# First block of a fused linear-attention and two-MLP kernel: weight decoding by steps, state update and split behind it, unit 4 begun in front of the block

## The chip, the cores and the metric

The kernel runs on one core of one Trainium2 chip. The metric is the device time of one execution in microseconds (us). Three runs of the kernel before took 947.99, 950.5 and 950.2 us, a median of 950.2 us.

## The reference

A recurrent linear attention is followed by two MLPs, in fp32:

```
state = 0                                    # [4 batches, 8 heads, 48, 48]
for t in range(768):
    y[t]  = r[t] @ (state + (u * k[t]) x v[t])
    state = w[t] * state + k[t] x v[t]       # w in 0.8 .. 0.95
x = y as [3072 tokens, 384]
h = x @ w_in;   x = elu(h) @ w_out           # 384 -> 2048 -> 384
h = x @ w_in2;  out = silu(h) @ w_out2       # 384 -> 2048 -> 384
```

## The kernel before

**Attention.** The 3072 tokens are cut into 24 units of 128 tokens (6 chunks of time by 4 batches). For each unit, VectorE (DVE) makes running products of w with two scans (`scan`, L160, and `scan_back`, L170), the product r*k (`products`, L222), and scaled copies of r and k (`q`, L237, and `kt`, L244). ScalarE (ACT) writes a check sum of the decays (`far`, L178), a copy of the whole decay (`whole_decay`, L183) and the diagonal of the attention matrix (`diag`, eight activations, L201, from the sums that `summed` takes on TensorE, L229). TensorE (PE) then makes the scores (`scores`, L287, two banks of PSUM), a transposed k (`ktok`, L253, copied out by ACT in `ktok_copy`, L259), the contribution of the old state (`past`, L342), the outer product for the new state (`outer`, L316) and the part within the unit (`within`, L361). DVE masks the scores (`masked`, L304). `update` brings the state forward (DVE L326 and L328, then ACT L330), and `split` writes the unit's output as two rounded parts xh (ACT L373) and xl (DVE L374).

**MLPs.** Weights and activations are held as a rounded part and a remainder, so each product is three matmuls. The first MLP runs in six blocks of four units (512 tokens); a block has 16 slots, one for each slice of 128 hidden channels. A slot f (function `slot`) issues nine matmuls into a bank `ph` (`hidden`, L443), the split of the slot before (gh on ACT L465, gl on DVE L466), the exponential and a ReLU on ACT (L450, L452), one half of a tick, g = max(...) on DVE (L459), the nine output matmuls of slot f-2 (`flush_out`, L474), and the other half of the tick. The banks `ph` are two, so the hidden matmuls of slot f+2 wait for g of slot f.

**Weights.** They come in as 64-bit floats and are decoded by hand in four steps for each slice: `w_load` (two DMAs of 384 KB into one of three staging buffers), `w_scale` (two activations, L405 and L407), `w_join` (two DVE operations, L414 and L416) and `w_split` (wh on ACT L428, wl on DVE L429). The first MLP's 16 slices are decoded during the first block: `w_tick` does a join and a scale in the first half of a slot, a split and a load in the second.

**Order.** All engines work through queues that the program writes by hand (`manual_schedule`). `dense_units` does units 0 to 3 with nothing beside them; while it runs, slices 0 to 2 are decoded. It ends with eight transposes that only keep PE busy (`keep_clock`, L617). The first block then runs, and its slots carry units 4 to 7, each as six steps (`round_ticks`: t0 to t5) spread over the half slots. Unit 4 is in `ALONE`: its preparation stands in `prep_rest`, in the first two half slots. In t5 of a unit stand past, outer, within, the next unit's ktok, then update, split and ktok_copy. The three remaining banks of PSUM go around between these: the scores of unit n+1 are written to the banks that the state update and the ktok_copy of unit n read.

Of the kernel before, what the change touches and what calls it, by code (L numbers as in the profile page):

```python
# [34 lines left out]
def kernel(  # L35
# [116 lines left out]
    def prep_steps(n):  # L152
# [61 lines left out]
        def products():  # L214
            if n >= SUMMED:
                return
            if n < BLOCKS[0]:
                rk = g_p.tile([RB, NP, L], F32, tag="gh", name="rk")
            else:
                rk = st["af"][0:RB, 0:NP * L].rearrange("p (j t) -> p j t", j=NP)  # L220
            st["rk"] = rk
            nc.vector.tensor_tensor(out=rk, in0=st["c"][:, 0], in1=st["c"][:, 1], op=ALU.mult)  # L222
# [165 lines left out]
    wh, wl = {}, {}  # L388
    halves, loaded, scaled, whole = [], [], [], []

# [28 lines left out]

    def w_split():  # L420
        if whole:
# [5 lines left out]
            h, l = (x.rearrange("p o c -> p (o c)") for x in (h, l))  # L427
            nc.scalar.activation(out=h, in_=t, func=ACTF.Copy)  # L428
            nc.vector.tensor_tensor(out=l, in0=t, in1=h.bitcast(F32), op=ALU.subtract)  # L429

# [105 lines left out]
    def round_parts(n, free=None):  # L536
# [11 lines left out]
        return pe, do  # L548

    def round_ticks(n):  # L550
        pe, do = round_parts(n)
# [35 lines left out]
        def t5():  # L587

            pe["past"]()
            pe["outer"]()  # L590
            pe["within"]()
            do("ktok")
            pe["update"]()
            pe["split"]()
            do("ktok_copy")
            load_unit(n + 2, "v")

        return [t0, t1, t2, t3, t4, t5]

    def dense_units():  # L600

# [4 lines left out]
                 for pool, tag, k in ((ps_o, "o", 3), (ps_h, "h", 2)) for _ in range(k)]  # L606
        sums_p = banks[2]

        def begin(n):
# [9 lines left out]
        for n in range(-1, count):  # L619
# [5 lines left out]
            if more:  # L625
# [6 lines left out]
                p["whole_decay"]()  # L632
                p["far"]()
                p["q"]()
                p["kt"]()
# [5 lines left out]
            if more:  # L641
                begin(n + 1)
                w_join()
            if n >= 0:
                pe[n]["masked"](0)
                pe[n]["masked"](1)
# [6 lines left out]
            if more:  # L653
                w_split()
                w_load()
# [7 lines left out]
            if n == KRAT:  # L663
                nc.sync.dma_start(u_sb, u.rearrange("h d -> (h d)").unsqueeze(0).to_broadcast([128, H * D]))
        keep_clock(8)
        pe[count - 1]["split"]()
        w_join()
        w_split()
        w_load()
        w_scale()  # L670
        pe[count - 1]["update"]()

    def prep_rest(at, n, p):

        if at == 1:
            p["bonus"]()
# [46 lines left out]
    def w_tick(part):  # L723

        if part == 0:
            w_join()
            w_scale()
        else:
            w_split()
            w_load()  # L730

    with tc.manual_schedule():
# [10 lines left out]
        setup()  # L743
        nc.scalar.activation(out=upper, in_=above_sb, func=ACTF.Copy)
        dense_units()

# [11 lines left out]
        for j, units in enumerate(BLOCKS):  # L758
            nt, final = units * L, j == len(BLOCKS) - 1
            ticks = [] if final else list(range(FIRST[j + 1], FIRST[j + 2]))  # L760
            todo, count, at = [], 6 * len(ticks), 0
            alone = prep_steps(ticks[0]) if ticks and ticks[0] in ALONE else None

            def tick(part):
# [5 lines left out]
                wait, end = DELAY if alone else 0, END if j == 0 else 2 * NF - 2  # L770
                while done < count and done * (end - wait) < (at - wait) * count:
                    if not todo:
                        todo.extend(round_ticks(ticks.pop(0)))
                    todo.pop(0)()
                    done += 1
                if j == 0 or final and f % 4 != 3:
                    w_tick(part)

            for f in range(NF):
# [112 lines left out]
    def all_weights(m):  # L892
        stage_open(2)
        w_start(m)
        for _ in range(NF):
            w_scale()
            w_join()
            w_split()
            w_load()
# [92 lines left out]
```

## Time and profile before

| what | value |
|---|---|
| runs of the kernel | 947.99, 950.5, 950.2 us; median 950.2 us |
| the profiled execution | 947.38 us, of which the span of the trace is 945.6 us |
| mean granted clock of PE | 0.981 |
| busy share of the span | PE 97%, DVE 52%, ACT 53%, POOL 14% |
| chain that ended last | PE 89%, DVE 6%, DMA 2%, ACT 2% |

Times within the trace count from the span's start. The dense units fill about the first 42.5 us, and the first block follows. In a timeline row the two leading numbers are start and duration; what stands in brackets is the idle time of the engine before it and what ended it. An operation's successor on the same engine can start a little before the operation's recorded end.

### The profile page before, as it was taken

The page shows a single profiled execution, that of the slowest core. Times are in us where ns is not written, and L with a number is a line of the kernel's source. Part 1 is how long each engine was busy: PE and PEld are TensorE (multiplying, and loading weights), DVE is VectorE, ACT ScalarE, POOL GpSimd, SP SyncE. Part 2 cuts the span into 40 slices and gives each one's busy share as a digit, 9 for nine tenths or more (in the row PEclk, how much of TensorE's full clock was granted, in tenths as well). Part 3 has the DMA queues.
Part 4 walks back from the last instruction along what each step waited for, and adds up shares of the span by engine and source line. Part 5 has one row for each costly group of instructions (what it writes and reads, how often), then busy time and mean ns, then how long its engine had stood idle before and what let it go on. Part 6 is the DMA issues. An engine that isn't in the chain of part 4 may idle for free.

```text
span 945.6 us, 15205 instructions
## 1 busy us (share of the span) xinstructions
PE 918.1 (97%) x6158; PEld 790.8 (84%) x6158; DVE 489.4 (52%) x726; ACT 502.4 (53%) x901; POOL 133.9 (14%) x101
## 2 busy tenths in 40 slices
PE   7779899999999999999999999999999999999996
PEld 7667688888888888888888899999999999999996
DVE  7798877776666776666378762212212212222211
ACT  6788866665655655555488963323323333333332
POOL 0000012443453334453000000000000000000000
PEclk8799999999999999999999999999999999999998
DMA  8644414222322221220245330100200200200001
GB/s 252 184 153 161 163 48 124 69 67 57 110 67 73 91 66 57 78 68 1 101 141 193 136 99 1 67 0 1 68 1 1 68 1 1 67 1 1 34 1 37
DMA packets 32222, 68.69 MB, mean 73 GB/s; under 512 B 3600, under 2 KB 13968, under 8 KB 32144
## 3 DMA queue, kind: packets, MB, share of 16 engines
q1 hardware_dynamic: 32144, 67.64, 22.5%
q8 instruction: 50, 0.82, 0.4%
q14 instruction: 28, 0.23, 0.1%
HBM read 58.19 MB, written 9.44 MB: 72 GB/s over the span
## 4 chain that ended last, share of the span: by engine, by line
PE 89%; DVE 6%; DMA 2%; ACT 2%; issue 1%; SPq 0%; DVEq 0%; ACTq 0%
PE ph L443 40%; PE po L482 21%; PE po L474 19%; PE sc L295 2%; PE y L361 2%; PE y L342 1%; DVE wst L414 1%; PE ktp L253 1%; DVE wl L429 1%; DVE wst L416 1%; DMA in_v<-in_v_tok_dram 1%; DVE am L304 1%; DVE gl L466 1%; PE upd L316 1%; DMA above_sb<-in_above_dram 1%
## 5 line engine op out<-in xcount | busy, mean ns | idle before, releaser
L466 DVE TENSOR_TENSOR gl<-g,gh 128x512 fp32r<-128x512 f32 x192 | 144.8, 754 | 313.5 <-ACT gh L465 313.3
L443 PE MATMUL ph<-xh,wh 128*128 128x512 f32 x576 | 227.6, 395 | 2.1 <-DVE g L459 2.1
L443 PE MATMUL ph<-xh,wl 128*128 128x512 f32 x576 | 227.4, 395 | 0.0
L443 PE MATMUL ph<-xl,wh 128*128 128x512 f32 x576 | 227.2, 394 | 0.0
L465 ACT ACTIVATE gh<-g 128x512 fp32r<-128x512 f32 x192 | 120.8, 629 | 153.7 <-PE po L482 109.7
L454 ACT ACTIVATE g<-ph 128x512 f32<-128x512 f32 x96 | 57.4, 598 | 137.8 <-PE ph L443 137.1
L482 PE MATMUL po<-wh,gl 128*128 128x384 f32 x384 | 129.5, 337 | 0.0
L482 PE MATMUL po<-wh,gh 128*128 128x384 f32 x384 | 129.3, 337 | 0.0
L482 PE MATMUL po<-wl,gh 128*128 128x384 f32 x384 | 128.9, 336 | 0.0
L443 PEld LDWEIGHTS ph<-xh,wl 128*128 128x128 f32 x576 | 108.7, 189 | 23.5
L443 PEld LDWEIGHTS ph<-xh,wh 128*128 128x128 f32 x576 | 109.1, 189 | 22.4 <-DVE g L459 2.5
L443 PEld LDWEIGHTS ph<-xl,wh 128*128 128x128 f32 x576 | 108.8, 189 | 19.5
L474 PE MATMUL po<-gh,wh 128*128 128x512 f32 x288 | 114.7, 398 | 0.0
L474 PE MATMUL po<-gl,wh 128*128 128x512 f32 x288 | 113.0, 392 | 0.0
L474 PE MATMUL po<-gh,wl 128*128 128x512 f32 x288 | 112.7, 391 | 0.0
L450 ACT ACTIVATE g<-ph 128x512 f32<-128x512 f32 x96 | 56.5, 589 | 52.2 <-PE ph L443 52.1
L459 DVE SCALAR_TENSOR_TENSOR g<-g,ph 128x512 f32<-128x512 f32 x96 | 65.4, 681 | 27.7 <-ACT g L452 27.1
L482 PEld LDWEIGHTS po<-wh,gh 128*128 128x128 f32 x384 | 72.2, 188 | 4.3 <-ACT x2s L493 0.2
L482 PEld LDWEIGHTS po<-wl,gh 128*128 128x128 f32 x384 | 72.1, 188 | 4.1
L482 PEld LDWEIGHTS po<-wh,gl 128*128 128x128 f32 x384 | 72.0, 188 | 0.0
L233 POOL TENSOR_TENSOR ql<-tq,qh 64x512 fp32r<-64x512 f32 (+1 forms) x30 | 42.7, 1423 | 167.1 <-ACT qh L232 166.0
L474 PEld LDWEIGHTS po<-gh,wh 128*128 128x128 f32 x288 | 54.5, 189 | 11.8 <-issue 0.8
(92 smaller groups left out, 1078.6 us busy)
## 6 DMA issues: line engine op xcount, KB each, us to landing
wst<-in_moe_w_in_dram SPq DMA_DIRECT2D x32, 384.0 KB, 3.2
wst<-in_moe_w_out_dram SPq DMA_DIRECT2D x32, 384.0 KB, 4.0
in_c<-in_rk_ch_dram SPq DMA_DIRECT2D x24, 448.0 KB, 3.8
in_w<-in_w_ch_dram SPq DMA_DIRECT2D x24, 226.2 KB, 2.7
in_v<-in_v_tok_dram SPq DMA_DIRECT2D x24, 224.0 KB, 3.1
x_d<-x2s SPq DMA_DIRECT2D x18, 256.0 KB, 2.4
xl<-x_d SPq DMA_DIRECT2D x6, 768.0 KB, 5.3
out_dram<-os SPq DMA_DIRECT2D x24, 192.0 KB, 2.0
```

Of the source, the lines that this page charges most:

```text
L233: nc.gpsimd.tensor_tensor(out=lo, in0=x, in1=hi.bitcast(F32), op=ALU.subtract)
L253: nc.tensor.transpose(p[:, j, :], st["kd"][:, j, :], ident[0:RB, 0:RB])
L295: nc.tensor.matmul(p[:, jj].rearrange("p e t -> p (e t)"), a[:, j, :], b[:, j].rearrange("p e t -> p (e t)"), start=i == 0, stop=i == len( ...
L361: nc.tensor.matmul(y[32 * base:32 * base + 32, blk // 4, :], vf[:, c:c + 32], st["a"][:, h // 2, h % 2, :], start=not ch and step == 0, st ...
L443: nc.tensor.matmul(ph, lhs, xt[rhs][:, kt, 0:nt], start=n == 0, stop=n == 3 * KT - 1)
L450: nc.scalar.activation(out=g, in_=ph, func=ACTF.Exp)
L454: nc.scalar.activation(out=g, in_=ph, func=ACTF.Silu)
L459: nc.vector.scalar_tensor_tensor(out=g, in0=g, scalar=-1.0, in1=ph, op0=ALU.mult, op1=ALU.max)
L465: nc.scalar.activation(out=gh, in_=g, func=ACTF.Copy)
L466: nc.vector.tensor_tensor(out=gl, in0=g, in1=gh.bitcast(F32), op=ALU.subtract)
L474: nc.tensor.matmul(po[ot][:, 0:nt], lhs, rhs, start=f == 0 and i == 0, stop=f == NF - 1 and i == 2)
L482: nc.tensor.matmul(po[t][:, 0:DM], lhs[:, sl], rhs["o", f], start=f == 0 and i == 0, stop=f == NF - 1 and i == 2)
```

## The change

1. **Weights.** `w_split` is cut into `w_high` (wh on ACT) and `w_low` (wl on DVE). In the first half of slot f, `w_tick` now does wh of slice f+2, the join of slice f+3, wl of slice f+2 and a load; in the second half it scales slice f+4. The slice that was split at the end of `dense_units` (slice 2) is split in slot 0; the load that followed it goes there too.
2. **Update and split.** The end of t5 (update, split, ktok_copy and a load of v) becomes a step t6 that is put off to the end of the same half slot, behind `w_tick`.
3. **Unit 4.** Its products, scan and sums stand in `dense_units` in front of the masking of unit 3, its scan_back and whole_decay behind `keep_clock`. Of its preparation only q, kt, far and diag stay in the first two half slots.
4. **Mask.** The copy that turns the loaded mask into `upper` on ACT moves from before the dense units to behind the `far` of unit 0.

```diff
-            if n < BLOCKS[0]:
+            if n <= BLOCKS[0]:
                 rk = g_p.tile([RB, NP, L], F32, tag="gh", name="rk")
...
-    def w_split():
+    def w_high():
...
             nc.scalar.activation(out=h, in_=t, func=ACTF.Copy)
+            rounded_w.append((t, h, l))
+
+    def w_low():
+        if rounded_w:
+            t, h, l = rounded_w.pop(0)
             nc.vector.tensor_tensor(out=l, in0=t, in1=h.bitcast(F32), op=ALU.subtract)
...
+    behind = []
+
+    def follow():
+        while behind:
+            behind.pop(0)()
...
             do("ktok")
+            behind.append(t6)
+
+        def t6():
             pe["update"]()
             pe["split"]()
             do("ktok_copy")
...
+                if n == -1:
+                    mask()
                 p["q"]()
...
+            if n == count - 1:
+                after["bonus"]()
+                after["products"]()
+                after["scan"]()
+                after["summed"](sums_p[:, count * H:(count + 1) * H])
             if n >= 0:
                 pe[n]["masked"](0)
...
         keep_clock(8)
+        after["scan_back"]()
+        after["whole_decay"]()
         pe[count - 1]["split"]()
         w_join()
-        w_split()
-        w_load()
         w_scale()
         pe[count - 1]["update"]()
...
+        if n == BLOCKS[0]:
+            if at == 1:
+                p["q"]()
+                p["kt"]()
+                load_unit(n + 2, "wc")
+                p["far"]()
+                p["diag"](0)
+            elif at == 2:
+                p["diag"](1)
...
         if part == 0:
+            w_high()
             w_join()
+            w_low()
+            w_load()
+        else:
             w_scale()
-        else:
-            w_split()
-            w_load()
...
                 while done < count and done * (end - wait) < (at - wait) * count:
+                    follow()
...
                 if j == 0 or final and f % 4 != 3:
                     w_tick(part)
+                follow()
```

DVE at the end of the dense units and in slot 0 (slice 2 is `wst_220`, slice 3 `wst_297`; unit 4's scans write `both_100`, its q and kt are `tq` and `tk`). Before, from wl of slice 2 to q of unit 4:

```order
L429 TENSOR_TENSOR wl2_0_575<-wst_220,wh2_0_574 128x768
L328 TENSOR_TENSOR packed3_108<-upd_522,whole_432 112x192
L222 TENSOR_TENSOR am_599<-in_c_338 112x512
L159 MEMSET seed_99 112x4
L160 SCALAR_TENSOR_TENSOR both_100<-in_w_336,seed_99 112x516
L166 TENSOR_SCALAR seed_99<-both_100 112x4
L168 RECIPROCAL seed_99<-seed_99 112x4
L170 SCALAR_TENSOR_TENSOR both_100<-in_w_336,seed_99 112x515
L414 SCALAR_TENSOR_TENSOR wst_297<-wst_297 128x768
L416 SCALAR_TENSOR_TENSOR wst_297<-wst_297 128x768
L459 SCALAR_TENSOR_TENSOR g_596<-g_596,ph_586 128x512
L237 TENSOR_TENSOR tq_620<-in_c_338,both_100 112x512
```

In the changed kernel, the same stretch:

```order
L328 TENSOR_TENSOR packed3_108<-upd_522,whole_432 112x192
L237 TENSOR_TENSOR tq_606<-in_c_338,both_100 112x512
L244 TENSOR_TENSOR tk_608<-in_c_338,both_100 112x512
L414 SCALAR_TENSOR_TENSOR wst_297<-wst_297 128x768
L416 SCALAR_TENSOR_TENSOR wst_297<-wst_297 128x768
L434 TENSOR_TENSOR wl2_0_622<-wst_220,wh2_0_621 128x768
L464 SCALAR_TENSOR_TENSOR g_603<-g_603,ph_593 128x512
L471 TENSOR_TENSOR gl_648<-g_603,gh_647 128x512
```

The product and both scans of unit 4 have left the stretch, and wl of slice 2 stands between the join of slice 3 and g of slot 0.

ACT in slot 0 of the changed kernel (the first row is the end of unit 3's state update, the next two the exponential and ReLU of slot 0; `am_539` is unit 4's diagonal and, in the fourth row, the scrap output of its check sum):

```order
L330 ACTIVATE state3_104<-packed3_108 48x4x48 x2
L455 ACTIVATE g_603<-ph_593 128x512
L457 ACTIVATE g_603<-g_603 128x512
L178 ACTIVATE am_539,sums_98<-both_100 112x1031
L198 ACTIVATE dg_615<-early_160 128x8
L201 ACTIVATE am_539<-ident_94,dg_615 128x128 x4
L428 ACTIVATE wh2_0_621<-wst_220 128x768
L201 ACTIVATE am_539<-ident_94,dg_615 128x128 x4
L405 ACTIVATE wst_399<-wst_399 128x768
L407 ACTIVATE wst_399<-wst_399 128x768
L470 ACTIVATE gh_647<-g_603 128x512
```

Before, wh of slice 2 stood in front of that state update; now five operations of slot 0 and unit 4 stand between.

DVE in slot 10, where t5 of unit 6 falls in the first half (`packed2_107` is its state, `xl` its split). Before:

```order
L466 TENSOR_TENSOR gl_1254<-g_1214,gh_1253 128x512
L326 TENSOR_TENSOR packed2_107<-upd_1273,packed2_107 112x192
L328 TENSOR_TENSOR packed2_107<-packed2_107,whole_915 112x192
L374 TENSOR_TENSOR xl_662<-y_1260,xh_661 128x3x128
L414 SCALAR_TENSOR_TENSOR wst_1084<-wst_1084 128x768
L416 SCALAR_TENSOR_TENSOR wst_1084<-wst_1084 128x768
```

In the changed kernel:

```order
L471 TENSOR_TENSOR gl_1250<-g_1207,gh_1249 128x512
L414 SCALAR_TENSOR_TENSOR wst_1103<-wst_1103 128x768
L416 SCALAR_TENSOR_TENSOR wst_1103<-wst_1103 128x768
L434 TENSOR_TENSOR wl12_0_1308<-wst_1004,wh12_0_1307 128x768
L326 TENSOR_TENSOR packed2_107<-upd_1269,packed2_107 112x192
L328 TENSOR_TENSOR packed2_107<-packed2_107,whole_910 112x192
L374 TENSOR_TENSOR xl_655<-y_1256,xh_654 128x3x128
```

Before, update and split stood ahead of the join of slice 13 (`wst_1084`); now the join of slice 13 (`wst_1103`) and wl of slice 12 stand ahead of them. The order of PE's matmuls is the same in both kernels, but for unit 4's sums.

## Rows read from the trace of the kernel before

**Rows 1.** Windows: busy time of each engine in stretches, granted PE clock, DMA share, GB/s.

```profile
42.50:60.00 17.50, 13.81 (x75) 11.21 (x75) 15.44 (x24) 15.76 (x33) 0.00 (x0) 0.90 0.43 147
60.00:80.00 20.00, 16.64 (x154) 12.49 (x153) 17.61 (x28) 16.82 (x33) 0.00 (x0) 0.91 0.52 166
80.00:100.00 20.00, 20.00 (x184) 16.05 (x182) 17.59 (x27) 18.41 (x36) 0.00 (x0) 1.00 0.48 161
100.00:118.00 18.00, 14.69 (x144) 11.17 (x145) 16.04 (x24) 15.46 (x31) 0.00 (x0) 0.91 0.46 159
118.00:946.00 828.00, 820.34 (x5194) 710.80 (x5194) 389.07 (x570) 406.83 (x700) 132.14 (x92) 1.00 0.18 57
```

**Rows 2.** Timeline of PE: its waits in the first block.

```profile
51.74 1.16 PE L287 MATMUL sc<-tq,tk 64*128 64x128 f32 x16 [3.46 <-DVE tk L244]
...
72.94 0.84 PE L287 MATMUL sc<-tq,tk 48*128 48x128 f32 x6 [1.70 <-ACT kt L259]
...
117.22 0.71 PE L287 MATMUL sc<-tq,tk 48*128 48x128 f32 x6 [1.25 <-ACT kt L259]
```

**Rows 3.** Windows of 3.4 us after two of these waits.

```profile
53.00:56.40 3.40, 3.40 (x11) 2.82 (x11) 3.36 (x6) 3.37 (x7) 0.00 (x0) 0.51 0.45 155
...
117.80:121.20 3.40, 3.40 (x21) 2.49 (x20) 2.99 (x5) 3.11 (x6) 0.00 (x0) 1.00 0.64 182
```

**Rows 4.** Chain of waits: nine output matmuls at either clock (start, duration).

```profile
73.78 3.69 PE po L474 x9
...
120.87 2.29 PE po L474 x9
```

**Rows 5.** Groups of DVE instructions from 42.4 to 118 us.

```profile
L429 DVE TENSOR_TENSOR wl<-wst,wh 128x768 fp32r<-128x768 f32 x11 | 10.5, 951 | 4.1 <-ACT wh L428 4.1
L414 DVE SCALAR_TENSOR_TENSOR wst<-wst 128x768 int32<-128x768 int32 x11 | 10.4, 946 | 0.0
...
L160 DVE TENSOR_TENSOR_SCAN both<-in_w,seed 112x516 f32<-112x516 f32 x4 | 4.9, 1234 | 0.2
...
L222 DVE TENSOR_TENSOR am<-in_c 112x512 f32<-112x512 f32 x4 | 2.7, 682 | 0.0
```

**Rows 6.** Timeline of DVE: scan of unit 1, with the wait before it.

```profile
9.86 1.23 DVE L160 TENSOR_TENSOR_SCAN both<-in_w,seed 112x516 f32<-112x516 f32 x1 [0.97 <-ACT am L178]
```

**Rows 7.** Timeline: end of the dense units, on DVE and PE.

```profile
36.73 1.34 DVE L304 COPY_PREDICATED am<-upper,early 128x512 f32<-128x512 int8 x2 [2.43 <-ACT am L201]
37.51 0.41 PE L361 MATMUL y<-am,in_v 128*32 128x128 f32 x4 [1.71 <-DVE am L304]
...
39.12 3.68 PE L617 MATMUL early<-ident 128*128 128x128 f32 x16
```

**Rows 8.** Timeline of ACT in slot 0.

```profile
44.59 0.72 ACT L330 ACTIVATE state<-packed 48x192 f32<-48x192 f32 x2
45.34 0.60 ACT L450 ACTIVATE g<-ph 128x512 f32<-128x512 f32 x1
45.97 0.63 ACT L452 ACTIVATE g<-g 128x512 f32<-128x512 f32 x1
...
48.20 1.05 ACT L178 ACTIVATE am<-both 112x1031 bf16<-112x1031 f32 x1
...
49.42 2.45 ACT L201 ACTIVATE am<-ident,dg 128x128 f32<-128x128 f32 x8
51.78 0.88 ACT L428 ACTIVATE wh<-wst 128x768 fp32r<-128x768 f32 x1
```

**Rows 9.** DMA issues: KB each, us from issue to landing.

```profile
wst<-in_moe_w_out_dram SPq DMA_DIRECT2D x32, 384.0 KB, 4.0
```

**Rows 10.** Timeline of DVE: g of slot 2; state update and split of unit 6.

```profile
65.22 0.68 DVE L459 SCALAR_TENSOR_TENSOR g<-g,ph 128x512 f32<-128x512 f32 x1
...
114.64 0.35 DVE L326 TENSOR_TENSOR packed<-upd,packed 112x192 f32<-112x192 f32 x1
...
116.77 0.56 DVE L374 TENSOR_TENSOR xl<-y,xh 128x384 fp32r<-128x384 f32 x1 [1.39 <-ACT xh L373]
```

More of the change, by code (lines that the diff above doesn't have):

```diff
@@ L388 @@
     wh, wl = {}, {}
-    halves, loaded, scaled, whole = [], [], [], []
+    halves, loaded, scaled, whole, rounded_w = [], [], [], [], []
     def w_load():
@@ L598, in round_ticks, with dense_units @@
         return [t0, t1, t2, t3, t4, t5]
-    def dense_units():
+    def dense_units(mask):
         count = BLOCKS[0]
@@ L607, in dense_units @@
         sums_p = banks[2]
+        after = prep_steps(count)
         def begin(n):
@@ L665, in dense_units @@
         keep_clock(8)
+        after["scan_back"]()
+        after["whole_decay"]()
         pe[count - 1]["split"]()
         w_join()
-        w_split()
-        w_load()
         w_scale()
         pe[count - 1]["update"]()
+        return after
     def prep_rest(at, n, p):
-        if at == 1:
+        if n == BLOCKS[0]:
[7 more added lines that the diff above has]
+                p["diag"](1)
+        elif at == 1:
             p["bonus"]()
@@ L725, in w_tick @@
         if part == 0:
+            w_high()
             w_join()
+            w_low()
+            w_load()
+        else:
             w_scale()
-        else:
-            w_split()
-            w_load()
     with tc.manual_schedule():
@@ L743 @@
         setup()
-        nc.scalar.activation(out=upper, in_=above_sb, func=ACTF.Copy)
-        dense_units()
+        first_alone = dense_units(
+            lambda: nc.scalar.activation(out=upper, in_=above_sb, func=ACTF.Copy))
         x2t = {}
@@ L761 @@
             todo, count, at = [], 6 * len(ticks), 0
-            alone = prep_steps(ticks[0]) if ticks and ticks[0] in ALONE else None
+            alone = None
+            if ticks and ticks[0] in ALONE:
+                alone = prep_steps(ticks[0]) if j else first_alone
             def tick(part):
@@ L897, in all_weights @@
             w_join()
-            w_split()
+            w_high()
+            w_low()
             w_load()
```

## The prediction

> **What bounds the kernel now.** I read the windows first. From 118 us to the end PE is busy 820.3 of 828 us at a granted clock of 1.00 [rows 1]; no engine but PE has a say there, and the change does not touch its matmuls. All that can move lies before 118 us. In the first block up to there, 75.5 us, DVE is busy 15.44 + 17.61 + 17.59 + 16.04 = 66.7 us, while PE pauses [rows 1]. The timeline of PE shows the pauses: 3.46 us before unit 4's scores, which wait for its kt on DVE, 1.70 us at unit 5's scores and 1.25 us at unit 7's, which wait for a bank of PSUM that ACT's copy of k must free [rows 2]. The last of these ends at 117.22 us, and behind it PE never waits for long. So the time is: when PE gets past unit 7's scores, plus a fixed rest of matmuls. What the change does elsewhere counts only if it moves that moment.
>
> A pause has a second price. After the 3.46 us one the granted clock of PE was 0.51, the 1.2 GHz level, in the next 3.4 us; after the 1.25 us one it stayed at 1.00 [rows 3]. Nine output matmuls took 3.69 us right after the 1.70 us pause and 2.29 us at full clock [rows 4]: 1.4 us lost by each such fall.
>
> I follow DVE and ACT in the order of their queues, each operation starting when its engine is free and its inputs are there, with the durations of the rows, and compare at the same operation.
>
> **The change part by part.**
>
> *Mask.* ACT copies the mask before anything of unit 0, and DVE waited 0.97 us for ACT's check sum of unit 0 [rows 6]. With the mask behind that check sum the wait goes: DVE's next scan starts when DVE is free. ACT's own later work waits for PE and for weights, so at most 0.97 us and at least nothing reaches the block; I take **-0.75**, near the row.
>
> *Unit 4 in front.* Product 0.68, two scans of 1.23 and some 0.3 of small operations, 3.45 us in all, leave DVE's stretch in the block [rows 5]. The product and scan fit into the 2.43 us that DVE waits for unit 3's diagonal; unit 4's sums fit PE's 1.71 us pause, where they also bring the eight transposes of keep_clock forward [rows 7]. Those took 3.68 us for 16 passes right after that pause [rows 7], 0.23 us a pass; the pause had lowered the clock as in [rows 3], and at the full one they would take half. If the filled pause keeps the clock up, hidden of slot 0 starts nearly 2 us sooner; of that 1.3 us arrive, since the exponential of slot 0 then has to wait for unit 3's state update on ACT, which ends about 43.6 us. Without a higher clock it is 0. I take **-1.3**, because the pause that went ahead of the fall is the one that is filled.
>
> *What takes its place.* In slot 0, DVE is through with q, kt and the join of slice 3 by 46.0 us (counted from 40.7, where unit 3's split lets it go: 3.8 us of joins, 0.35 of state, 1.4 of q and kt). It then meets wl of slice 2, which needs wh on ACT. ACT can start the exponential at 45.0 and has 0.60 + 0.63 + 1.05 + 0.2 + half of 2.45 + 0.88, with small overlaps 4.45 us, up to the end of wh [rows 8]: 49.4. DVE stands idle 3.4 us, with g of slot 0 queued behind, and hidden of slot 2 waits for both parts. After g, gl waits 1.8 us for gh, since the rest of the diagonal (1.2) and two scalings stand before it on ACT. Before, DVE's idle time in this stretch was 0.96 and 1.10 us (part of the 4.1 us before wl [rows 5]). So 3.2 us of new idle time eat the 3.45 us; by g of slot 2, at 65.3 us in this count against 65.22 [rows 10], nothing is gained: **+0.1**.
>
> *Decoding by steps.* Each later slot holds the same 3.95 us of weight and gate work on DVE; wl now stands before g instead of behind. In slots 3 and 6, where ACT has half a diagonal (1.2) in front of wh, wl waits 0.7 us; the old waits of wl behind ACT's state and copy, about 0.8 us, go, but in the two slots the count ends 0.4 us later each time: **+0.8**. The loads are issued later by a step too: that of slice 5 behind wl of slice 2. They landed in 4.0 us [rows 9], and the count has 5 us or more until their scaling: 0, and if they collide with the loads of unit 6 issued behind them, up to +1.
>
> *Update and split behind.* For units 4 and 5, t5 falls in the second half of a slot, where only scalings on ACT precede: the update is not delayed much. For unit 6 it falls in the first half of slot 10. The update stood at 114.64, its split at 116.77, and ACT's copy of k freed unit 7's scores at 117.22 [rows 2, 10]. Now a join (2 x 0.95, 1.87 net) and wl (0.95, but already done before in the old order) come first: **+2.0**. Behind them PE has only out of slot 8 to do, so unit 7's scores wait some 4 us instead of 1.25. By the two falls above that pause lowers the clock, which costs **+1.4** (0 if PE's banks free in two steps and the clock holds).
>
> *Nothing:* the moved mask copy (0.31 us) in ACT's free time; the loads of unit 6's w and rk on SP, which have ten slots' time.
>
> **Sum.** -0.75 - 1.3 + 0.1 + 0.8 + 2.0 + 1.4 = +2.25, say **+2.2 us**. The profiled execution took 947.38 us (span 945.6), so it becomes 949.6. It lies 2.8 us under the median of the runs shown, 950.2; against that median I predict **952.4**.
>
> **Rivals.**
>
> *DVE keeps its lead (faster).* If ACT's part of slot 0 is shorter than I count, so that wl of slice 2 waits under 1 us, the 3.45 us moved off DVE arrive at unit 7's scores. With the new 3.2 us of idle time gone and the clock held the sum is 2.25 - 3.2 - 1.4 = -2.35; if the waits of slots 3 and 6 go as well, -3.15, giving 947.1 to 947.9; with part of DVE's 4.1 us of waits for wh [rows 5] gone too, 945. For it: the longest pause of PE in the block, 3.46 us [rows 2], is the one that unit 4's early start attacks, and kt is ready before PE asks. Against it: DVE is 88% busy there [rows 1], so what follows a removed wait is the next one.
> The Trainium skill, Perfetto Trace Analysis, section Optimization Strategy, says to find the gaps of the engine that matters, see what they wait for, and make that start sooner. By that rule the 3.46 us gap and its fall of the clock, 4.9 us, would come off, 945.3 us against the median; this trace bears out that the gap waits for kt, but not that nothing else is due at the same time.
>
> *No front gain (slower).* One mechanism: PE's front stays at the half clock through keep_clock and the mask's 0.75 us is lost to the weights' DMA, so hidden of slot 0 starts as before, 42.46, and unit 6's late update is not paid for: +0.1 + 0.8 + 2.0 + 1.4 = +4.3, 954.5. It decides as soon as the two front terms give less than 1.5 us together. For it: the clock was low in that place; against it: the filled pause.
>
> *Front and back cancel (same).* The clock holds behind unit 7's scores, and the sum is +0.8: 951.0.
>
> **How the numbers follow.** A difference under 0.3% (2.85 us) can't be told from none. The forecast, with the case in which front and back cancel, lies within that: 0.48 (forecast 0.30, cancelling 0.18). No front gain, or a forecast whose open terms (+1 for loads, 0 for the clock in front) fall badly: 0.35. DVE keeps its lead by over 2.85 us: 0.17. The range, 947.0 to 956.0, reaches from the weaker form of the faster rival to the forecast with 0 for both front gains and +1 for loads (952.4 + 3.05 = 955.5); I leave 0.2 outside.
>
> **What would show it.** Right: PE's wait before unit 4's scores gone; DVE idle 2 to 3.5 us before wl of slice 2 in slot 0, released by ACT's wh; g of slot 2 within 2 us of 65; unit 7's scores waiting for ACT's copy of k after 117.5 us, for over 2 us, with a clock near 0.5 behind; PE full from there on. The front is right if the first hidden matmuls start near 40.5 us. Wrong: DVE without idle time in slots 0 and 1, or unit 7's scores before 115 us; then DVE kept its lead. Hidden of slot 0 at 42 us or later would speak for the slower rival.

## The result, and the profile after

Nine runs of each on one chip: 955.19 us with the change (952.21 to 956.69), 950.09 us before (946.89 to 951.65). The ratio is 1.0058, interval [1.0044, 1.0073]: **slower by 0.6%**, some 5.5 us by the ratio and 5.1 us between the medians, more than the 0.3% that can be told from no change. The profiled execution took 955.26 us, its span is 953.5 us (945.6 before), the mean granted clock 0.971 (0.981). The profiled execution of the kernel before, 947.38 us, was one of its quicker ones, so the 7.9 us between the two spans, which the traces below account for, are more than the change costs on average. PE's share of the chain fell from 89% to 84%, DVE's rose from 6% to 7% and ACT's from 2% to 4%.

The windows of the changed kernel (busy time of PE, PEld, DVE, ACT, POOL, then the granted clock of PE, DMA share, GB/s), to be held against [rows 1]:

```profile
42.50:60.00 17.50, 14.02 (x64) 10.83 (x63) 12.06 (x18) 14.28 (x30) 0.00 (x0) 0.77 0.38 123
60.00:80.00 20.00, 17.09 (x147) 12.98 (x146) 16.99 (x25) 16.18 (x31) 0.00 (x0) 0.77 0.39 132
80.00:100.00 20.00, 20.00 (x180) 16.06 (x180) 16.48 (x25) 17.56 (x33) 0.00 (x0) 1.00 0.50 165
100.00:118.00 18.00, 15.56 (x145) 12.03 (x144) 17.03 (x26) 15.09 (x29) 0.00 (x0) 0.91 0.50 168
118.00:126.00 8.00, 5.25 (x17) 4.03 (x17) 3.20 (x6) 3.84 (x7) 0.00 (x0) 0.65 0.49 166
126.00:954.00 828.00, 819.72 (x5187) 709.87 (x5185) 387.64 (x566) 405.43 (x697) 131.82 (x92) 1.00 0.18 56
```

The last row is the full stretch of [rows 1], 828 us with 819.7 of PE, but it begins at 126 us and not at 118. The two spans differ by 7.9 us, so nearly the whole difference arises in front of 126 us. In the first two windows the clock is 0.77 (0.90 and 0.91 before), and DVE, which lost work, idles 5.4 of 17.5 us. PE's waits in the block, which answer to [rows 2] (start, duration; idle time in front and what ended it):

```profile
50.76 0.47 PE L448 MATMUL ph<-xh,wh 128*128 128x512 f32 x1 [2.56 <-DVE g L464]
...
54.68 1.87 PE L229 MATMUL sums<-u_ch,am 112*128 112x2 f32 x8 [0.91 <-ACT kt L259]
...
71.24 0.49 PE L287 MATMUL sc<-tq,tk 64*128 64x128 f32 x2 [1.02 <-DVE packed L326]
...
73.61 1.22 PE L287 MATMUL sc<-tq,tk 48*128 48x128 f32 x6 [1.89 <-ACT kt L259]
...
108.94 0.47 PE L448 MATMUL ph<-xh,wh 128*128 128x512 f32 x1 [1.85 <-DVE g L464]
...
119.05 0.49 PE L287 MATMUL sc<-tq,tk 64*128 64x128 f32 x2 [1.63 <-DVE packed L326]
121.23 1.22 PE L287 MATMUL sc<-tq,tk 48*128 48x128 f32 x6 [1.69 <-ACT kt L259]
```

Unit 4's scores no longer wait for kt on DVE (3.46 us before), but a wait of 2.56 us for g of slot 0 stands shortly behind them, at hidden of slot 2. The last pause is now double, 1.63 us for the state update and 1.69 us for the copy of k, and ends at 121.23 us (117.22 before). Behind it PE ran at 1.2 GHz, where [rows 3] had 1.00:

```profile
122.00:124.00 2.00, 2.00 (x8) 1.49 (x6) 0.57 (x1) 1.40 (x3) 0.00 (x0) 0.50 0.42 155
124.00:126.00 2.00, 2.00 (x7) 1.48 (x5) 0.12 (x1) 0.00 (x0) 0.00 (x0) 0.50 0.00 0
```

From unit 7's scores to the next output matmuls PE needed 127.47 - 121.23 = 6.24 us; before it was 120.80 - 117.22 = 3.58. So of the 7.9 us, 4.0 are the later end of the pause, 2.7 the clock behind it, and 0.8 two waits of PE at 540 and 552 us, 0.23 and 0.59 us, that the trace of before does not have; 0.4 us are left over.

Why the update was late: DVE in slot 10, against [rows 10].

```profile
113.87 0.68 DVE L464 SCALAR_TENSOR_TENSOR g<-g,ph 128x512 f32<-128x512 f32 x1
...
115.92 0.95 DVE L414 SCALAR_TENSOR_TENSOR wst<-wst 128x768 int32<-128x768 int32 x1
116.90 0.96 DVE L416 SCALAR_TENSOR_TENSOR wst<-wst 128x768 int32<-128x768 int32 x1
117.78 0.95 DVE L434 TENSOR_TENSOR wl<-wst,wh 128x768 fp32r<-128x768 f32 x1
118.65 0.35 DVE L326 TENSOR_TENSOR packed<-upd,packed 112x192 f32<-112x192 f32 x1
...
120.78 0.56 DVE L374 TENSOR_TENSOR xl<-y,xh 128x384 fp32r<-128x384 f32 x1 [1.39 <-ACT xh L373]
```

The first row is g of slot 9, which in the kernel before was

```profile
112.07 0.68 DVE L459 SCALAR_TENSOR_TENSOR g<-g,ph 128x512 f32<-128x512 f32 x1
```

The update starts 4.0 us later than before. From g of slot 9 to the update DVE needs 4.78 us, with the join now ahead of the update as well as wl, where it needed 2.57: that is 2.2 us. The other 1.8 us DVE brings with it, since g of slot 9 is late by that much already. Where they come from, two of DVE's groups show (busy time, mean ns of one operation; idle time in front). The first fence is the changed kernel from 42.4 to 126 us; the rows that answer are wl in [rows 5] and, in the second fence, gl of the kernel before, both from 42.4 to 118 us:

```profile
L434 DVE TENSOR_TENSOR wl<-wst,wh 128x768 fp32r<-128x768 f32 x11 | 10.5, 955 | 5.4 <-ACT wh L428 5.4
...
L471 DVE TENSOR_TENSOR gl<-g,gh 128x512 fp32r<-128x512 f32 x11 | 7.5, 686 | 5.3 <-ACT gh L470 5.3
```

```profile
L466 DVE TENSOR_TENSOR gl<-g,gh 128x512 fp32r<-128x512 f32 x10 | 6.8, 682 | 0.0
```

Before, gl never waited for gh: wl stood between g and gl and covered the time in which ACT makes gh. Now wl stands ahead of g, and gl waits 5.3 us in all, 3.8 of them by 118 us.

The front, against [rows 6, 7]: scan of unit 1 on DVE; then PE.

```profile
8.88 1.23 DVE L160 TENSOR_TENSOR_SCAN both<-in_w,seed 112x516 f32<-112x516 f32 x1
```

```profile
34.84 1.87 PE L229 MATMUL early<-u_ch,rk 112*128 112x2 f32 x8
36.64 2.52 PE L361 MATMUL y<-am,in_v 128*32 128x128 f32 x32
39.09 3.37 PE L633 MATMUL early<-ident 128*128 128x128 f32 x16
42.21 0.48 PE L448 MATMUL ph<-xh,wh 128*128 128x512 f32 x1
```

The mask's 0.97 us wait is gone and unit 4's sums fill the 1.71 us pause. But PE's matmuls behind them are slow: y of unit 3 took 2.52 us in place of 0.41 and 1.07 us, and hidden of slot 0 came 0.25 us sooner, not 1.3 or 2. The clock of that stretch, after and then before:

```profile
36.00:39.00 3.00, 3.00 (x36) 2.18 (x35) 2.84 (x6) 1.42 (x5) 0.00 (x0) 0.50 0.89 223
```

```profile
36.00:39.00 3.00, 1.29 (x32) 0.94 (x32) 1.90 (x3) 2.09 (x7) 0.00 (x0) 1.00 0.99 271
```

In the kernel before PE had the full clock there and was busy 1.29 of 3 us; in the changed kernel it was busy throughout at half the clock, and the same work ended within 0.25 us of the same moment. The pause is not what made the clock high: in the run with the mask alone (below) the same matmuls waited as long, y took as long as in the changed kernel, and the clock was 0.50:

```profile
36.68 2.53 PE L361 MATMUL y<-am,in_v 128*32 128x128 f32 x32 [1.73 <-DVE am L304]
```

```profile
36.00:39.00 3.00, 2.32 (x32) 1.52 (x32) 1.80 (x3) 1.26 (x4) 0.00 (x0) 0.50 0.93 198
```

### The profile page after: what moved, and what is told of

Read it like the earlier page. It is cut to its first block, busy times and chain, and to the rows that moved or that the text cites. A ratio compares the mean times of both kernels' runs of the same rounds, so it can differ in the third digit from the quotient of the medians.

```text
span 953.5 us, 15208 instructions
## 1 busy us (share of the span) xinstructions
PE 926.9 (97%) x6158; PEld 796.9 (84%) x6158; DVE 490.9 (51%) x726; ACT 503.1 (53%) x901; POOL 133.6 (14%) x101
## 4 chain that ended last, share of the span: by engine, by line
PE 84%; DVE 7%; ACT 4%; DMA 2%; issue 2%; SPq 0%; ACTq 0%; DVEq 0%
PE ph L448 38%; PE po L487 21%; PE po L479 17%; PE sc L295 2%; PE y L361 2%; DVE wl L434 2%; PE y L342 1%; DMA wst<-in_moe_w_out_dram 1%; DVE wst L414 1%; DVE wst L416 1%; DVE g L464 1%; ACT gh L470 1%; PE ktp L253 1%; PE sc L287 1%; DVE am L304 1%
## 5 line engine op out<-in xcount | busy, mean ns | idle before, releaser
L464 DVE SCALAR_TENSOR_TENSOR g<-g,ph 128x512 f32<-128x512 f32 x96 | 65.3, 681 | 26.4 <-ACT g L457 26.2
L479 PEld LDWEIGHTS po<-gh,wl 128*128 128x128 f32 x288 | 55.0, 191 | 12.0
```

Of the source, the lines that this page charges most:

```text
L464: nc.vector.scalar_tensor_tensor(out=g, in0=g, scalar=-1.0, in1=ph, op0=ALU.mult, op1=ALU.max)
L479: nc.tensor.matmul(po[ot][:, 0:nt], lhs, rhs, start=f == 0 and i == 0, stop=f == NF - 1 and i == 2)
```

## The experiments

All ratios are to the kernel before, run on the same chip; a gain or loss in us is worked out from the ratio unless medians are named. Each expectation names a theory and a rival to it. The start of g on DVE, one for each slot of the first block, shows how far each profiled execution had come (us):

| kernel | ratio [interval] | slot 1 | slot 6 | slot 8 | slot 10 | slot 11 | slot 15 |
|---|---|---|---|---|---|---|---|
| before | 1 | 57.91 | 90.91 | 106.31 | 119.10 | 124.13 | 141.03 |
| the change | 1.0058 [1.0044, 1.0073] | 57.51 | 92.98 | 108.11 | 121.25 | 130.93 | 147.79 |
| update and split at once | 1.0051 [1.0034, 1.0068] | 57.66 | 93.77 | 110.47 | 123.62 | 130.77 | 147.59 |
| slice 2 split in front | 1.0054 [1.0040, 1.0068] | 57.69 | 93.65 | 108.80 | 121.96 | 131.63 | 148.49 |
| unit 4 back in the slots | 1.0063 [1.0045, 1.0081] | 58.32 | 94.43 | 109.56 | 123.74 | 132.88 | 149.70 |
| decoding back | 1.0046 [1.0030, 1.0062] | 57.70 | 92.88 | 109.31 | 122.07 | 131.10 | 148.72 |
| update behind, alone | 1.0060 [1.0045, 1.0074] | 58.22 | 92.81 | 109.23 | 121.98 | 130.69 | 148.33 |
| decoding by steps, alone | 1.0054 [1.0038, 1.0070] | 57.88 | 93.95 | 110.65 | 123.93 | 131.02 | 147.80 |
| unit 4 in front, alone | 1.0006 [0.9996, 1.0015] | 58.42 | 91.42 | 106.80 | 119.59 | 125.43 | 143.07 |
| mask, alone | 0.9991 [0.9979, 1.0003] | 57.93 | 90.94 | 106.34 | 119.16 | 124.99 | 142.60 |
| decoding and update back | 0.9986 [0.9973, 0.9999] | 58.12 | 91.12 | 106.52 | 119.29 | 124.31 | 141.16 |
| copy of k at once | 1.0032 [1.0018, 1.0047] | 56.84 | 91.42 | 106.04 | 119.24 | 127.00 | 143.82 |
| before, copy of k first | 0.9954 [0.9940, 0.9967] | 58.69 | 91.17 | 106.05 | 118.77 | 123.77 | 139.01 |
| ACT in another order | 0.9908 [0.9892, 0.9924] | 54.94 | 88.01 | 102.89 | 115.57 | 120.59 | 135.57 |

### One part undone: four runs

**Update and split at once.**

```diff
             do("ktok")
-            behind.append(t6)
+            t6()
```

> The changed kernel with its second part undone: update, split and copy of k of a unit stand at the end of step t5 again, ahead of that half slot's decoding. Theory (late update): the state update of unit 6 starts near 116.5 us instead of 118.65, unit 7's scores end their wait near 119 us instead of 121.23, at most one stretch of half clock follows instead of two, and 3 to 5 us come back: 950.2 to 952.2 us where the changed kernel took 955.2. Rival (DVE is late already): the queue of DVE is 1.8 us behind by slot 8 and the late update only takes the place of other waits; then under 1 us comes back, 954.2 us or more.

1.0051: next to nothing came back. The rival held. The update of unit 6 came at 118.28 us, not near 116.5, because g of slot 8 was already 2.4 us later than in the changed kernel. With the update ahead of the decoding again, gl waits longer for gh, 7.0 us up to 118 us where the changed kernel had 3.8, so one wait took the place of the other. Unit 7's scores still ended their wait at 120.87 us with half clock behind:

```profile
118.69 0.48 PE L287 MATMUL sc<-tq,tk 64*128 64x128 f32 x2 [0.41 <-DVE packed L326]
120.87 1.22 PE L287 MATMUL sc<-tq,tk 48*128 48x128 f32 x6 [1.70 <-ACT kt L259]
```

**Slice 2 split in front.**

```diff
         w_join()
+        w_high()
+        w_low()
+        w_load()
         w_scale()
...
             w_join()
-            w_low()
-            w_load()
+            if rounded_w:
+                w_low()
+                w_load()
```

> The changed kernel, but slice 2 is split (and the load behind it issued) at the end of the dense units as before; slot 0 has no wh and no wl. Theory (idle in slot 0): DVE's 3.57 us of idle time in front of wl of slice 2 goes, its lead of 2 to 2.6 us reaches g of slot 2 (62.2 to 63 us instead of 64.80) and two thirds of it unit 7's scores; 953.5 us or less, against 955.2. Rival (the idle time was free): PE's order sets the pace there, g of slot 2 comes within 0.7 us of 64.80, and the time is within 0.8 us of the changed kernel.

1.0054, g of slot 2 at 65.01 us: the rival's result. DVE's 3.57 us of idle time was free. With it gone PE ran into a longer wait right behind, 4.19 us for ACT's copy of k where the changed kernel had 0.91:

```profile
54.86 1.86 PE L229 MATMUL sums<-u_ch,am 112*128 112x2 f32 x8 [4.19 <-ACT kt L259]
```

So ACT's queue set slots 0 and 1, not DVE's.

**Unit 4 back in the slots** (product, scans and sums leave the dense units and stand in `prep_rest` again; the main lines of the edit).

```diff
...
-            if n == count - 1:
-                after["bonus"]()
-                after["products"]()
-                after["scan"]()
-                after["summed"](sums_p[:, count * H:(count + 1) * H])
...
-        after["scan_back"]()
-        after["whole_decay"]()
...
-        if n == BLOCKS[0]:
...
-        elif at == 1:
+        if at == 1:
...
```

> The changed kernel with its third part undone: unit 4 is prepared in the first two half slots again. Theory (the early start is worth little, since its time falls into slot 0's idle time): DVE's idle time in front of wl of slice 2 shrinks from 3.57 us to under 1, scores of unit 4 wait 2 to 3.5 us again with a half clock behind, and g of slot 2 comes 0.5 to 2 us later: 955.5 to 957 us. Rival (the early start hurts, because the filled pause keeps PE at half clock in front): hidden of slot 0 comes no later than 42.3 us and the time falls by 0.5 to 1.5 us, 953.7 to 954.7.

1.0063 [1.0045, 1.0081]: in the direction of the theory, but the interval covers the 1.0058 of the changed kernel. Scores of unit 4 wait 2.57 us again and g of slot 2 comes 0.84 us later, as the theory has it. The third part was worth little in this setting.

**Decoding back.**

```diff
-            w_high()
             w_join()
-            w_low()
-            w_load()
+            w_scale()
         else:
-            w_scale()
+            w_high()
+            w_low()
+            w_load()
```

(and slice 2 split in front as above.)

> The changed kernel with its first part undone: in each slot join and scale in the first half, wh, wl and load in the second, and slice 2 split at the end of the dense units; late update, early unit 4 and mask stay. Theory (decoding by steps costs DVE its lead, and puts wl ahead of the late update): the waits of wl for wh in slots 0, 3 and 6 go, the update of unit 6 has only a join ahead of it, and 2 to 4 us come back: 951.2 to 953.2 us. Rival (only the late update counts): the join alone still puts the update behind, and under 1 us comes back.

1.0046: 1.1 us back of the 2 to 4 expected, not told apart from the changed kernel. The theory fell here too; the update, behind a join, came at 119.46 us.

Not one of the three parts undone gives the time back (in four runs, with the split of slice 2 by itself). Either the cost lies elsewhere, or more than one part is able to cause it alone. The next runs tell that apart.

### One part alone, on the kernel before: four runs

Each leaves the other three parts as they were before; for the decoding the edit is the reverse of the last diff, for unit 4 of the one ahead of it.

**Update and split behind, alone.**

```diff
             do("ktok")
-            pe["update"]()
-            pe["split"]()
-            do("ktok_copy")
-            load_unit(n + 2, "v")
+            behind.append(t6)
...
```

(`t6` holds the four lines that are taken out, and is called at the end of the half slot, as in the change.)

> The kernel before with the second part alone: update, split and copy of k behind the half slot's decoding (there a join and a scaling). Theory (one long pause at unit 7's scores is paid in full by whichever part makes DVE late): the update of unit 6 starts 1.9 us later, at 116.5 us, unit 7's scores come at 119 us, PE falls to half clock behind, and the time rises by 3.5 to 5 us: 953.6 to 955.1 where the kernel before takes 950.1. Rival (each part costs by itself, and costs add): a third of the whole change, 1 to 2 us, 951.1 to 952.1.

1.0060: as much as the whole change. The update of unit 6 starts 4.7 us later than before, more than the 1.9 us expected, since PE and DVE were late by slot 8 already (g of slot 8 2.9 us):

```profile
119.38 0.35 DVE L326 TENSOR_TENSOR packed<-upd,packed 112x192 f32<-112x192 f32 x1
```

**Decoding by steps, alone.**

> The kernel before with the first part alone: in the first half of a slot wh, join, wl and load, in the second the scaling; slice 2 split in slot 0. Theory (wl stood behind g and covered the time that ACT takes for gh; now wl stands ahead of g and gl waits 0.76 us for gh in most slots): g of slot 8 comes at 108 us or later instead of 106.31, unit 7's scores at 118.5 or later with half clock behind, and the time rises by 3 to 5 us, 953.1 to 955.1. Rival (only the late update makes the long pause): g of slot 8 within 1 us, time within 1.5 us of the kernel before.

1.0054: again as much as the whole. gl's wait for gh (groups of DVE, 42.4 to 126 us) is 8.1 us, 7.4 of them by 118 us, from none, and g of slot 8 comes 4.3 us late:

```profile
L434 DVE TENSOR_TENSOR wl<-wst,wh 128x768 fp32r<-128x768 f32 x11 | 10.5, 953 | 1.1 <-ACT wh L428 1.1
...
L471 DVE TENSOR_TENSOR gl<-g,gh 128x512 fp32r<-128x512 f32 x11 | 7.6, 688 | 8.1 <-ACT gh L470 8.1
```

**Unit 4 in front, alone.**

> The kernel before with the third part alone: unit 4 begun in the dense units. Theory (it takes 3.45 us off DVE in the block and slice 2 is still split in front, so DVE gets ahead): scores of unit 4 start by 49 us without a wait, g of slot 2 near 63 us, unit 7's scores no later than before, 117.2 us; 946 to 949.5 us against 950.1. Rival (PE stays at half clock in front and what DVE wins is lost at the next wait): within 1 us of the kernel before, or above.

1.0006 [0.9996, 1.0015]: the rival. Scores of unit 4 do not wait, yet g of slot 2 comes at 65.72 us and not near 63.

**Mask, alone.**

```diff
-        nc.scalar.activation(out=upper, in_=above_sb, func=ACTF.Copy)
...
                 p["far"]()
+                if n == -1:
+                    mask()
```

> The kernel before with the fourth part alone: the mask's copy behind the check sum of unit 0. Theory (the front is paced by what follows, the block by DVE and the clock): the 0.97 us wait goes at the second scan, hidden of slot 0 starts 0 to 0.8 us sooner than 42.46, and the time changes by -0.8 to 0, 949.3 to 950.1. Rival (a shift of the front moves where the clock falls): the time rises by over 0.5 us though nothing in the block waits longer for DVE or ACT.

0.9991 [0.9979, 1.0003]: no difference that can be told. Hidden of slot 0 came at 42.6 us, no sooner.

The four alone add up to 0.60 + 0.54 + 0.06 - 0.09 = 1.11%; together they cost 0.58%. **The two harmful parts do not add: each one alone is enough to bring on a long pause at unit 7's scores and the half clock behind it.** With the update behind alone the pause ends at 121.97 us, with the decoding by steps alone at 121.18, in the changed kernel at 121.23, and the clock from 118 to 126 us is 0.68, 0.66 and 0.65. Part of it is evened out before the pause: at g of slot 8 the two parts alone are 2.9 and 4.3 us late, the changed kernel, with 3.8 us of gl's wait instead of 7.4, only 1.8.

### Both harmful parts undone

```diff
-            behind.append(t6)
+            t6()
...
-            w_high()
             w_join()
-            w_low()
-            w_load()
+            w_scale()
         else:
-            w_scale()
+            w_high()
+            w_low()
+            w_load()
```

> The changed kernel with its first and second part undone, so that only the mask and the early unit 4 are left. Theory (either part alone brings on the same long pause at unit 7's scores, so undoing one gives back next to nothing and undoing both gives all): g of slot 11 at 124 to 125.5 us instead of 130.93, and 4.5 to 6 us come back: ratio to the kernel before 0.998 to 1.001. Rival (the early unit 4 or the mask carries a share that the single runs hid): ratio 1.002 or more.

0.9986 [0.9973, 0.9999], g of slot 11 at 124.31 us: all of it came back, as the theory has it. That settles where the loss came from. It leaves why the early unit 4 brings so little: g of slot 0 is 2.0 us sooner than before, g of slot 1 is not. DVE and PE in slots 0 and 1 of this kernel:

```profile
52.91 0.96 DVE L434 TENSOR_TENSOR wl<-wst,wh 128x768 fp32r<-128x768 f32 x1 [4.52 <-ACT wh L428]
```

```profile
56.59 1.87 PE L229 MATMUL sums<-u_ch,am 112*128 112x2 f32 x8 [5.81 <-ACT kt L259]
```

The 3.46 us wait of [rows 2] is gone, and a wait of 5.81 us for ACT stands behind it. ACT was never idle here from 42.58 to 56.6 us, and wh of slice 3 and the copy of k stood behind unit 4's check sum, diagonal and the scalings.

### The copy of k, which frees the second bank

**At once, in the changed kernel.**

```diff
             do("ktok")
+            do("ktok_copy")
             behind.append(t6)
...
             pe["split"]()
-            do("ktok_copy")
```

> The changed kernel, but ACT's copy of the next unit's transposed k stands right behind its transposes, in front of the half slot's decoding; update and split stay behind. Theory (the bank that this copy frees is the second half of the long pause): unit 7's scores wait for the state update, 119.05 us, and not again for the copy, so PE goes on 1.7 us sooner, and a half clock stretch of the two may go; 1.7 to 4 us less than the changed kernel, ratio to the kernel before 1.0015 to 1.004. Rival (the bank of the state update alone makes the pause, and the DVE queue behind it sets the rest): under 0.8 us less, ratio 1.005 or more.

1.0032 [1.0018, 1.0047]: 2.5 us less than the changed kernel by the two ratios, with update and split still behind the decoding. The theory held in the time. The scores wait for the state update last, and go on 4.1 us sooner (117.13 against 121.23 us), more than the 1.7 expected, since g of slot 8 is 2.1 us sooner too; a double pause and half clock remain (0.66 from 118 to 126 us):

```profile
114.99 0.48 PE L287 MATMUL sc<-tq,tk 64*128 64x128 f32 x2 [1.20 <-ACT kt L259]
117.13 1.22 PE L287 MATMUL sc<-tq,tk 48*128 48x128 f32 x6 [1.66 <-DVE packed L326]
```

**First, in the kernel before.**

```diff
             do("ktok")
+            do("ktok_copy")
             pe["update"]()
             pe["split"]()
-            do("ktok_copy")
```

> The kernel before, but in step t5 the copy of the next unit's transposed k stands in front of update and split, where ACT waits 0.68 us for the state update anyway; nothing else is changed. Theory (the last pause of the block sets the time): the 1.25 us pause at 117.22 us goes, and the 1.70 us one at 72.94 us with its half clock; the second is eaten by the wait for g at 107 us, so 1.2 to 3 us less: ratio to the kernel before 0.997 to 0.9987. Rival (DVE's queue, not the bank, sets when g of slot 10 comes): the pauses go, g of slot 10 stays at 119 us and the ratio is 0.9995 or more.

0.9954 [0.9940, 0.9967]: **one line moved wins 4.4 us** by the ratio (the medians, 944.18 and 949.6 us, lie 5.4 apart), more than the 1.2 to 3 us expected. The pause at unit 7's scores is gone, and the clock is full behind:

```profile
115.26 0.71 PE L287 MATMUL sc<-tq,tk 64*128 64x128 f32 x8
```

```profile
118.00:126.00 8.00, 8.00 (x42) 6.47 (x41) 7.60 (x11) 6.34 (x11) 0.00 (x0) 1.00 0.21 70
```

g of slot 10 moved by only 0.3 us, as the rival said, but this execution had started the block later (g of slot 1 at 58.69 us, 0.8 later than before), and by slot 15 it is 2.0 us ahead. The spans of the two profiles differ by 2.4 us, less than the medians. The runs of before spread over 5.1 us here (946.95 to 952.01), those of this kernel over 1.3 us (943.78 to 945.09). That the pauses cost a fall of the clock in some runs and not in others would explain both. The mean granted clock, recorded for every run, leans that way: of the 18 runs of before, the three at 0.981 to 0.983 took 946.95 to 947.22 us, the nine at 0.974 to 0.977 took 948.68 to 952.01. It does not show at which pause the clock fell.

### ACT's queue in slots 0 and 1

Mask and early unit 4 stay, decoding and update are as before, the copy of k is first; on top of that:

```diff
-            if n in ALONE:
+            if n in ALONE and n != BLOCKS[0]:
...
                 load_unit(n + 2, "wc")
+            elif at == 3:
                 p["far"]()
                 p["diag"](0)
-            elif at == 2:
+            elif at == 4:
+                p["ktok"]()
+                p["ktok_copy"]()
                 p["diag"](1)
...
+                if j == 0 and at == 3:
+                    w_join()
+                elif j == 0 and at == 4:
+                    w_scale()
+                    w_tick(1)
-                if j == 0 or final and f % 4 != 3:
+                elif j == 0 or final and f % 4 != 3:
                     w_tick(part)
```

> The mask and the early unit 4 of the change, decoding and update in place as before, the copy of k in front of update and split as in the last run, and ACT's queue of slots 0 and 1 in another order: unit 4's check sum and the first half of its diagonal stand behind wh of slice 3 and the exponential of slot 1, its own copy of k behind them, then the second half and the scaling of slice 5. Theory (with unit 4 early, ACT is the bound of slots 0 and 1: it is never idle from 42.6 to 56.6 us, and DVE waits 4.52 us for wh of slice 3): wh of slice 3 comes near 48.6 us instead of 52.01, g of slot 1 at 55.4 to 56.2 us instead of 58.12, and 1 us or more of that is left at g of slot 10, by 117.8 us; ratio to the kernel before 0.991 to 0.9942. Rival (DVE's and ACT's work of the later slots sets when the block ends, whatever the lead): g of slot 8 within 0.7 us of the 106.05 us of the run with the copy first, and the ratio 0.9945 to 0.9965, no better than that run's 0.9954.

0.9908 [0.9892, 0.9924], medians 941.25 against 950.18 us: **faster than both kernels, by 8.7 us than the one before**, a little more than the theory's 0.991. DVE and PE in slots 0 and 1, and g of slot 10:

```profile
49.23 0.96 DVE L434 TENSOR_TENSOR wl<-wst,wh 128x768 fp32r<-128x768 f32 x1 [1.02 <-ACT wh L428]
...
54.94 0.68 DVE L464 SCALAR_TENSOR_TENSOR g<-g,ph 128x512 f32<-128x512 f32 x1
...
115.57 0.68 DVE L464 SCALAR_TENSOR_TENSOR g<-g,ph 128x512 f32<-128x512 f32 x1
```

```profile
53.77 1.05 PE L229 MATMUL sums<-u_ch,am 112*128 112x2 f32 x8 [3.14 <-ACT kt L259]
```

DVE's wait for wh fell from 4.52 to 1.02 us. Against the run with decoding and update back, 3.2 us are won at g of slot 1, 3.6 at slot 8 and 3.7 at slot 10. Of the last two the copy of k accounts for 0.3 us if its run is held against before as it stands, for 1.0 to 1.1 if both are counted from g of slot 1. So 2.6 to 3.4 us of the lead are kept: in this pair of runs the queues of DVE and ACT set the pace of the block, and a lead in its front lasts.

## Why the prediction was right or wrong

The time lay within the range, 947.0 to 956.0 us, and on the side forecast, but the likeliest case, +2.2 us, was too small: a loss of 0.58% can be told from no change. The rival "no front gain" gave 954.5 us and came nearest. That the range held is partly luck: its upper end allows for front gains of 0, close to the 0.25 us that came, and for 1 us of trouble with the loads, and what took the place of that trouble were other terms that the sum had too small. By the steps:

- **Mask, -0.75.** The wait went [rows 6], and nothing of it arrived: alone 0.9991, hidden of slot 0 no sooner.
- **Unit 4 in front, -1.3: this step failed.** It took the pause for the cause of the low clock that followed. At 36 to 39 us the clock was 1.00 with the pause in the kernel before, 0.50 with the pause in the run with the mask alone, and 0.50 with PE busy in the changed kernel. Hidden of slot 0 gained 0.25 us in the pair, and alone the part gave 1.0006. Over all traces the size of the front's gain stays open: in the seven kernels with both front parts hidden of slot 0 starts between 41.21 and 42.60 us, in the four with neither between 42.41 and 43.19, never near the 40.5 that was to show the step right. "Hidden of slot 0 at 42 us or later would speak for the slower rival" was the right sign: 42.21.
- **What takes its place, +0.1: right.** DVE's idle time in front of wl of slice 2 was 3.57 us (3.4 counted), gl's wait 1.68 (1.8), g of slot 2 came at 64.80 (65.3):

```profile
49.05 0.96 DVE L434 TENSOR_TENSOR wl<-wst,wh 128x768 fp32r<-128x768 f32 x1 [3.57 <-ACT wh L428]
...
52.29 0.69 DVE L471 TENSOR_TENSOR gl<-g,gh 128x512 fp32r<-128x512 f32 x1 [1.68 <-ACT gh L470]
```

  What the count did not see is that the idle time was no price at all: taking it away (slice 2 in front) changed nothing, because ACT was the bound behind it.
- **Decoding by steps, +0.8: mis-sized.** Alone it costs 0.54%, 5.1 us. In the changed kernel g of slot 2 is 0.4 us ahead of before and g of slot 9 is 1.8 us late: 2.2 us lost in between. There wl waits for wh 0.56, 0.66 and 0.57 us in slots 3, 5 and 6, where two waits of 0.7 were counted. The count forgot what wl had covered where it stood: gl's waits for gh, 1.4 us in that stretch, 5.3 from 42.4 to 126 us, 8.1 with the decoding alone. The loads were costed at 0, with up to +1 held open; ACT waited 1.5 us for them, at 70 and 92 us, and no run shows what of that reached PE.
- **Update and split behind, +2.0 and +1.4.** Place and mechanism are as predicted: unit 7's scores wait until 121.23 us, 1.63 us for the state update and 1.69 for ACT's copy of k, at half clock behind. Slot 10 itself adds 2.2 us to the update, near the 2.0 of the count; that the update came 4.0 us later is what DVE brought along. The clock cost 2.7 us and not 1.4, since the nine hidden matmuls of slot 10 and the scores on both sides of them all ran slow.
- **The sum itself.** Terms were added. The runs show two parts of 5.1 and 5.7 us that together, with the other two, cost 5.5 us. Either is enough for the long pause at unit 7's scores, and together they make DVE less late ahead of it (1.8 us at slot 8) than each does alone (4.3 and 2.9).
- **DVE keeps its lead** did not come about in the change, but its price was about right: where ACT's queue was put in order, 2.6 to 3.4 us of the front's lead were kept. The Trainium skill, Perfetto Trace Analysis, section Optimization Strategy, which gave 945.3 us in the prediction, tells the reader to see what a gap waits for and make that start sooner. These traces agree with it only when it is applied again to the wait that follows: the 3.46 us gap was gone in eight kernels here, the change among them, and the time fell by more than 0.3% only in the one in which the next wait, ACT's 5.81 us, was shortened as well and the copy of k stood first.

## What to carry to other kernels

Before an operation is moved out of an in-order queue, look at what it covered there, not only at what it waits for in its new place. When undoing one part of a change gives nothing back, try parts alone and in pairs: causes that each suffice can't be found one at a time. And where an engine waits for a bank, look at where the operation that frees it stands in the other engine's queue: here one copy, put into time in which ACT waited anyway, won 0.46%, and no part of the change by itself won anything that can be told from nothing.

## What was not expected of the hardware

The same pause did not always cost the clock. Before unit 7's scores PE waited 1.25 us in the kernel before, 1.23 us with unit 4 alone and 1.27 us with the mask alone. In the 8 us from 118 us on the granted clock was 1.00 in the first, 0.79 in the others. With both harmful parts undone PE even paused twice there, 1.00 and 1.70 us, and the clock stayed at 1.00 (before; unit 4 alone; mask alone; both undone):

```profile
118.00:126.00 8.00, 8.00 (x40) 6.26 (x41) 7.55 (x11) 6.85 (x11) 0.00 (x0) 1.00 0.25 70
```

```profile
118.00:126.00 8.00, 8.00 (x37) 6.14 (x36) 6.82 (x9) 6.19 (x9) 0.00 (x0) 0.79 0.34 91
```

```profile
118.00:126.00 8.00, 8.00 (x33) 6.15 (x34) 6.83 (x10) 6.21 (x10) 0.00 (x0) 0.79 0.28 76
```

```profile
118.00:126.00 8.00, 8.00 (x41) 6.32 (x40) 7.56 (x11) 6.89 (x11) 0.00 (x0) 1.00 0.25 72
```

What tells them apart is open. It sets g of slot 11 back by 0.8 us (from slot 10: 5.03, 5.84, 5.83 and 5.02 us), so a pause of this size has a price that can't be read from one profile. And a busy PE was not always at the full clock: in the changed kernel's front, from 36 to 42 us, it was busy 6.00 of 6.00 us with small matmuls at 0.50 to 0.52.

The Trainium skill, TensorE: Matmul & The Clock Gate, Part 1, The HAM clock gate, says that activity releases the throttle, and that where this falls varies from run to run of one kernel. No two traces here are of one kernel, so the second is not shown; the rows above, of four kernels with nearly the same work in that place, are in keeping with it. The first alone does not explain the front, where a busy PE stayed at half clock.
